# Loads of two heads spread over the projection of v, and sums of x moved past a seam

## The chip, the cores and the metric

The kernel runs on one core of one Trainium2 chip. The metric is the device time of one execution in microseconds (us). The core has five engines that run their own instruction queues and meet by semaphores: TensorE (PE, matmuls into the eight banks of PSUM), VectorE (DVE), ScalarE (ACT), GpSimd (POOL) and SyncE (SP). In this kernel SP computes nothing: its queue issues nearly all transfers between memory and SBUF, one after the other. Sixteen DMA engines carry them out.

## The reference

The input x has 2048 rows and D = 1024 columns. Two attention blocks with 32 heads of 32 columns work on it, and a gate mixes them row by row:

```python
g = _sigmoid((x * gate_w).sum(-1, keepdims=True))
a = _A_ref(x, A_wqkv, A_wo)      # linear attention: pq @ (pk^T v), over pq @ sum(pk)
b = _B_ref(x, B_wqkv, B_wo)      # softmax(q k^T / sqrt(32)) v for each head
return g * a + (1 - g) * b
```

Both blocks first project x by a 1024 x 3072 weight to q, k and v, and finish with a 1024 x 1024 weight. In block A, `phi` makes positive features pq and pk of q and k. All inputs and outputs are float32.

## The kernel before

**Precision.** Every large operand is split into a high and a low part (`split`: a cast on ACT at L293, the rest by a subtraction on DVE at L294), and each product is three matmuls (`three`, L152, L155, L157). A matmul of 128 x 128 by 128 x 512 is the unit of work on TensorE.

**Stage 1, block B's projections.** The rows of x are taken in two halves, J = 0 and J = 1. For each, eight v passes (`v_pass(J, k, ...)`, k = 0 to 7) project 1024 rows to the first 512 columns of v into all eight banks. Eight quads (`quad`) then make q and k, each a 2 x 2 block product by seven products instead of eight, which needs sums and differences of blocks of x (`sides`, four subtractions on DVE at L372 to L375, and `split_sides`, which splits them) and of the weights. The fourth result of `sides`, L375, goes to one of four tiles that also hold results of a quad until `qk<-mid` stores have read them. The results q, k and v go to tensors in memory, `qk` and `v`.

**The seam.** While the last quad of half 0 runs, the generator `change()` (L605) is advanced step by step between its products and prepares half 1: it loads weights of v again, splits the first pieces of x and, in its last step, makes `sides(raw_x1[0], 0)`. The last quad's own last addition on DVE is at L483; it reads the bank of the seventh product, bank 1, which v pass 0 of half 1 fills last. The loop from L628 runs the passes of half 1, and after each pass it issues sums, splits and loads for later passes on DVE, ACT and SP.

**Stage 2, three streams beside each other.** From L921 on, a planner (the loop at the end of the kernel) keeps a modelled clock for each engine and picks the next piece of work from the streams `linear()` (L926), `maxima()` (L1111), `heads_()` and `output()`. All instructions of an engine are queued in the order in which they are picked.

`linear()` goes through units. A unit is one tile of 128 rows (t = 0 to 15) for a chunk of columns: 8 steps k of three matmuls. The first chunk is ("v", 1), the second 512 columns of v of block B, and its 16 units are called unit 0 to 15 here; unit 16 begins block A's k and v. x comes for each unit in two halves of four steps; a half is a pair of transfers (high and low, `big<-xs` or `xh<-xs`, 256 KB each) into one of three places, so half m + 3 is issued when half m has been used (`load_half`). Half m belongs to unit m // 2. At the end of a unit of v, ACT copies its bank (L355) and SP stores it (`v<-mid`).

`maxima()` computes the scores of a head once to find the maximum of each row: one matmul (L1127) and one reduction on DVE (L1132) for each of 64 tiles. Its bulk lies in units 6 to 14, about one matmul to a step. `heads_()` computes the scores again, transposed, with the exponential on ACT (L1301 and L1304); it begins with unit 16.

Head 0 and head 1 need q, k and v in SBUF. `load_q(h, j, j1)` and `load_k(h, j)` issue three transfers each (`big<-qk`, high and low parts of 32 partitions) and, for heads 0 and 1, `memset`s on POOL. `load_head(h)` (L1098) issues all 18 of a head, `load_v(h)` one (`mid<-v`):

```python
            if n == 0:
                load_head(0)
                load_v(0)
            if n == 1:
                load_head(1)
                load_v(1)
```

`gate()` (L487) makes g. Each `next` sums one row tile of x on DVE (L495, a product with `zrep`, which holds the gate's weights) and issues the load of the next row tile (`big<-in_x`, 512 KB). The first `next` loads the weights and row tile 0; the seventeenth sums row tile 15 and goes on to the exponential on ACT (L497) and three small steps on DVE. `linear()` calls it once in each unit of v, at step k = 4, and a second time in unit 15.

In unit 15, as each step of v's weights has been used, the weights of the next chunk are split into their place: a cast on ACT at L728, a subtraction on DVE at L730, from raw tiles loaded by `in_a_wqkv` transfers in pairs.

Of the kernel before, what the change touches and what calls it, by code (L numbers as in the profile page):

```python
# [47 lines left out]
def kernel(  # L48
# [22 lines left out]
    NK = D // P  # L71
    HK = NK // 2
    NT = S // P
    NJ = S // C
# [6 lines left out]
    def f32(ap):  # L81
        return ap.bitcast(F32)
# [37 lines left out]
    def big_tile(i, dtype):  # L120
        return sb.tile([P, S], dtype, name=f"big{i}")
# [39 lines left out]
    def use(eng, cost, *after):  # L161

        T[eng] = max(T[eng], *after, 0.0) + cost
        return T[eng] + LATENCY[eng]

    def dma(to, of):

        T["sp"] = max(T["sp"], T["pe"]) + DMA_ISSUE
        nc.sync.dma_start(to, of)  # L169
# [122 lines left out]
    def split(hi, lo, src, eng):  # L292
        nc.scalar.copy(hi, src)  # L293
        eng.tensor_sub(lo, src, f32(hi))  # L294
# [38 lines left out]
    def xpiece(J, name, p, i):  # L333
        return side_x(J, name, p)[:, i * C:(i + 1) * C]
# [13 lines left out]
    raw_x1 = [raw_a, raw_b, raw_a, raw_b]  # L348
# [20 lines left out]
    def sides(raws, i):  # L369

        r11, r12, r21, r22 = raws
        nc.vector.tensor_sub(r11, r12, r11)  # L372
        nc.vector.tensor_sub(r12, r22, r12)
        nc.vector.tensor_sub(r22, r22, r11)
        nc.vector.tensor_sub(t4_raw[i], r21, r22)  # L375

    def split_sides(raws, J, i):
        r11, r12, _, r22 = raws
        for name, raw in (("T1", r11), ("T2", r22), ("T3", r12)):
            split(xpiece(J, name, 0, i), xpiece(J, name, 1, i), raw, nc.vector)  # L380
# [106 lines left out]
    def gate():  # L487
        xn = halves_of(big_tile(12, F32))
        junk = halves_of(big_tile(13, F32))[0]
        dma(zrep, bass.AP(tensor=gate_w.tensor, offset=gate_w.offset, ap=[[0, P], [1, D]]))  # L490
        for t in range(NT):
            dma(xn[t % 2], x[t * P:(t + 1) * P, :])
            yield
            use("dve", 1.2)
            nc.vector.scalar_tensor_tensor(junk, xn[t % 2], 1.0, zrep, op0=ALU.mult, op1=ALU.mult,  # L495
                                           accum_out=g_sb[:, t:t + 1])
        nc.scalar.activation(g_sb, g_sb, AF.Exp, scale=-1.0)  # L497
        nc.vector.tensor_scalar_add(g_sb, g_sb, 1.0)
        nc.vector.reciprocal(g_sb, g_sb)
        nc.vector.tensor_scalar(omg_sb, g_sb, -1.0, 1.0, op0=ALU.mult, op1=ALU.add)  # L500

    def halves_of(t):
        return [t[:, i * D:(i + 1) * D] for i in range(2)]
# [49 lines left out]
    def load_pair(raws, J, i):  # L553
        for k in (2 * i, 2 * i + 1):
            for jj in range(2):
                load_x(raws, J, jj, k)
# [48 lines left out]
    def change():  # L605

        load_wv_again(range(NK - 1))
        split_x(raw_x1[0], 1, 0, 0)
        yield
        load_wv_again([NK - 1])  # L610
        split_x(raw_x1[0], 1, 1, 0)
        yield
        split_x(raw_x1[0], 1, 0, 1)
        yield
        split_x(raw_x1[0], 1, 1, 1)
        yield
        split_x(raw_x1[1], 1, 0, 2)
        split_x(raw_x1[1], 1, 1, 2)
        yield
        sides(raw_x1[0], 0)  # L620
        split_x(raw_x1[1], 1, 0, 3)
        split_x(raw_x1[1], 1, 1, 3)
        yield
# [4 lines left out]
    for k in range(NK):  # L628
        v_pass(1, k, V_BANKS[1])
        if k == 0:  # L630
            split_sides(raw_x1[0], 1, 0)
            load_pair(raw_x1[2], 1, 2)
            sides(raw_x1[1], 1)
        elif k == 1:
            split_sides(raw_x1[1], 1, 1)
            load_pair(raw_x1[3], 1, 3)
        elif k == 2:
            for kk in (4, 5):
                for jj in range(2):
                    split_x(raw_x1[2], 1, jj, kk)  # L640
            sides(raw_x1[2], 2)
        elif k == 3:
            for kk in (6, 7):
                for jj in range(2):
                    split_x(raw_x1[3], 1, jj, kk)
            sides(raw_x1[3], 3)
            split_sides(raw_x1[2], 1, 2)
            load_quad(raw_a, 0)
            for _ in spill(1, "X12"):
                pass  # L650
        elif k == 4:
            split_sides(raw_x1[3], 1, 3)
            load_quad(raw_b, 1)
        elif k == 5:
            quad_w = quad_weights(raw_a, 1, 0)
            next(quad_w)
            next(quad_w)
        elif k == 6:
            for _ in quad_w:
                pass  # L660
# [265 lines left out]
    def linear():  # L926
        extra = iter(())
        gates = gate()
        for n, (i, t) in enumerate(units):
            kind, c = chunks[i]  # L930
            follow = chunks[i + 1] if i + 1 < len(chunks) else None
# [13 lines left out]
            lin_kind[0] = kind  # L945
            if (kind, c, t) in (("q", 1, 2), ("q", 1, 8), ("o", 0, 2), ("o", 0, 8)):
                load_mix()
            if n == 0:
                load_head(0)
                load_v(0)  # L950
            if n == 1:
                load_head(1)
                load_v(1)
            for k in range(NK):
                yield lambda: ended(w_left[k], w_ready[k], xp_ready.get(2 * n + k // HK, 0.0))
                need(w_left[k])
                stat = [xstat_lin(n, k, p) for p in range(2)]
                for m, _ in enumerate(three(ps, stat, (wpart(k, 0), wpart(k, 1)), k)):
                    lin_pe(1.0)
                    if m < 2:  # L960
                        yield always
                store_mix()
                if kind == "v" and k == NK // 2:
                    next(gates, None)
                    if t == NT - 1:
                        next(gates, None)
                if k % HK == HK - 1:
                    load_half(2 * n + k // HK + 3)
                if k == 0 and n + 7 == len(units) and not o_main[0]:
                    load_o(0)  # L970
                if k == 1 and n + 1 == len(units):
                    assert finished[0] >= H - 2
                    need(pr_left[extra_pr[2]])
                    xo_t[0] = big_tile(PR[extra_pr[2]], F32R)
                    split_o(0, slice(0, NK - 1))
                if k == NK // 2 and n + 1 == len(units) and over["head"]:
                    split_o(1, slice(0, NK - 1))
                if k == NK - 1:
                    yield from extra
                if follow and follow[0] == "o":  # L980
                    if t == NT - 1:
                        w_left[k].clear()
                        yield lambda: 0.0 if mixed.count((k // HK, follow[1])) == 8 * HK else None
                        load_wa(follow[1], k)
                    continue
                if follow and t == NT - 2 and k == 0:
                    yield lambda: None if mix_here or stores else 0.0
                if follow and t == NT - 2 and k < min(LEAD_W, NK):
                    coming_w.append(load_w(*follow, k, LEAD_W + 1))
                if follow and t == NT - 1 and k >= lag:  # L990
                    renew(k - lag)
# [80 lines left out]
    def load_q(h, j, j1=0):  # L1072

        g, r = divmod(h, 4)
        j1 = max(j + 1, j1)
        q, sl = q_cols(h, j, j1), slice(j * C, j1 * C)
        if h < (2 if j else 3):
            nc.gpsimd.memset(f32(q[3 * DH:, :]), 0.0)  # L1078
        else:
            dma(f32(q[3 * DH:3 * DH + 2, :]), f32(q[3 * DH + 2:3 * DH + 4, :]))  # L1080
        for b, p in enumerate((0, 0, 1)):
            dma(f32(q[b * DH:(b + 1) * DH, :]), qk_d[0][p][g][r * DH:(r + 1) * DH, sl])
        for i in range(j, j1):
            q_ready[h][i] = max(T["pe"] + 8.0, T["sp"] + 5.0)

    def load_k(h, j):

        g, r = divmod(h, 4)
        k = k_stack[h % 2]
        if h < 2 and j == 0:  # L1090
            nc.gpsimd.memset(f32(k[3 * DH:, :]), 0.0)
            nc.gpsimd.memset(f32(k[3 * DH:3 * DH + 2, :]), 1.0)
        sl = slice(j * C, (j + 1) * C)
        for b, p in enumerate((0, 1, 0)):
            dma(f32(k[b * DH:(b + 1) * DH, sl]), qk_d[1][p][g][r * DH:(r + 1) * DH, sl])
        k_ready[h][j] = max(T["pe"] + 6.0, T["sp"] + 4.0)

    def load_head(h):  # L1098
        load_q(h, 0)
        load_q(h, 1, NJ)  # L1100
        for j in range(NJ):
            load_k(h, j)

    def v_tile(h):
        return mid[(2, 12)[h % 2]].rearrange("p (t d) -> p t d", d=DH)
# [1 line left out]
    def load_v(h):  # L1107
        c, o = divmod(h * DH, C)
        dma(v_tile(h), v_d[c][:, :, o:o + DH])
# [613 lines left out]
```

## Time and profile before

| what | value |
|---|---|
| median of 3 runs | 2865.99 us (2862.7 to 2868.45) |
| time of the profiled execution | 2866.15 us |
| its span, first to last instruction | 2864.4 us |
| mean granted clock of TensorE | 0.995 |
| TensorE busy | 2825.9 us, 99% of the span |
| DVE, ACT, POOL busy | 2233.2, 1595.8, 1909.2 us |
| mean DMA rate | 150 GB/s |

The profile gives for a group of instructions the line, the engine, the operation and out<-in by tile names; a bracket `[4.32 <-DVE mid L483]` says that the engine stood idle for 4.32 us before this instruction and what released it. A row of the timeline starts with the start and the duration in us; `x18` means that it merges 18 instructions. `SPq` is SP's queue, and the durations there are those of issuing, not of the transfer. A matmul's own duration (0.39 us) is longer than its share of TensorE, since matmuls overlap; the spacing of starts is what counts.

### The profile page before, as it was taken

The numbers are of one execution on the slowest core, as the hardware profiler recorded it, in microseconds if no ns is written. First come the engines' busy times: TensorE is split into PE (matmuls) and PEld (weight loads), VectorE is DVE, ScalarE is ACT, GpSimd is POOL, SyncE is SP. The second block draws the span as 40 slices with busy tenths as digits, with TensorE's granted clock in tenths as the row PEclk, the third lists the DMA queues.
The fourth block names the chain that finished last, engine by engine and source line by source line (L and its number), as shares of the span: only waits on it lengthen the run. The fifth ranks groups of instructions, "written<-read, shape, count | busy, mean of one in ns | idle before, by whom it ended". The sixth has DMA issues, their size and how long they took to land.

```text
span 2864.4 us, 46550 instructions
## 1 busy us (share of the span) xinstructions
PE 2825.9 (99%) x15944; PEld 2058.1 (72%) x15944; DVE 2233.2 (78%) x3659; ACT 1595.8 (56%) x2994; POOL 1909.2 (67%) x894
## 2 busy tenths in 40 slices
PE   9999988899999999999999999999999999999999
PEld 8878877667766776677767777777676766676787
DVE  7767755788888888888888888788888887887522
ACT  5334320366676667666766666566666666666400
POOL 0000010299999999999999999889889888885000
PEclk9999999999999999999999999999999999999999
DMA  8767768533343434333434344455656454634542
GB/s 278 245 214 222 224 202 272 191 87 99 100 133 98 104 100 129 93 96 96 127 107 101 100 122 137 143 173 171 201 174 188 134 163 136 161 108 133 196 151 78
DMA packets 376713, 428.56 MB, mean 150 GB/s; under 512 B 105006, under 2 KB 210734, under 8 KB 376476
## 3 DMA queue, kind: packets, MB, share of 16 engines
q1 hardware_dynamic: 362876, 412.47, 46.9%
q0 software_dynamic: 13600, 13.11, 3.3%
q8 instruction: 127, 2.08, 0.3%
q14 instruction: 110, 0.90, 0.1%
HBM read 298.06 MB, written 112.98 MB: 144 GB/s over the span
## 4 chain that ended last, share of the span: by engine, by line
PE 90%; DMA 2%; SPq 0%; DVE 0%; ACT 0%; issue 0%; ACTq 0%; DVEq 0%
PE bank L1301 17%; PE bank L1127 16%; PE bank L1458 16%; PE bank L152 13%; PE bank L155 13%; PE bank L157 13%; PE bank L1192 1%; PE bank L906 1%; DMA big<-wa 0%; PE bank L795 0%; DMA big<-xs 0%; DMA xh<-xs 0%; SPq L169 0%; DMA big<-qk 0%; PE bank L1184 0%; DMA big<-in_x 0%
## 5 line engine op out<-in xcount | busy, mean ns | idle before, releaser
L1393 POOL TENSOR_TENSOR big<-big,big 128x512 f32<-128x512 f32 (+2 forms) x694 | 1644.2, 2373 | 118.1 <-ACT big L1304 75.5
L1132 DVE TENSOR_REDUCE mx<-bank 128x1 f32<-128x512 f32 x2048 | 1306.8, 683 | 270.6 <-PE bank L1127 266.0
L1304 ACT ACTIVATE big<-bank 128x512 f32<-128x512 f32 x2048 | 1179.2, 601 | 436.3 <-PE bank L1301 367.6
L1301 PE MATMUL bank<-big,big 128*128 128x512 f32 x1888 | 742.5, 395 | 8.3 <-ACT mid L355 7.9
L1127 PE MATMUL bank<-big,big 128*128 128x512 f32 x1888 | 737.9, 392 | 2.8 <-DMA big<-qk 2.8
L152 PE MATMUL bank<-big,big 128*128 128x512 f32 x1600 | 627.4, 392 | 9.6 <-DMA big<-xs 5.2
L155 PE MATMUL bank<-big,big 128*128 128x512 f32 x1600 | 625.4, 391 | 0.0
L157 PE MATMUL bank<-big,big 128*128 128x512 f32 x1596 | 624.0, 391 | 0.3 <-DMA big<-xs 0.3
L1458 PE MATMUL bank<-big,mid 128*32 128x512 f32 x4096 | 454.1, 593 | 0.0
L1301 PEld LDWEIGHTS bank<-big,big 128*128 128x128 f32 x1888 | 354.0, 188 | 134.9 <-issue 47.8
L1127 PEld LDWEIGHTS bank<-big,big 128*128 128x128 f32 x1888 | 354.2, 188 | 77.9 <-issue 3.2
L152 PEld LDWEIGHTS bank<-big,big 128*128 128x128 f32 x1600 | 301.6, 189 | 77.1 <-DMA big<-xs 6.4
L157 PEld LDWEIGHTS bank<-big,big 128*128 128x128 f32 x1596 | 300.7, 188 | 64.9 <-DMA big<-xs 2.4
L155 PEld LDWEIGHTS bank<-big,big 128*128 128x128 f32 x1600 | 301.9, 189 | 63.0 <-DVE big L294 0.2
L1458 PEld LDWEIGHTS bank<-big,mid 128*32 128x32 f32 x4096 | 142.6, 110 | 265.2 <-issue 265.2
L1078 POOL MEMSET big<- 32x512 f32 (+1 forms) x4 | 3.7, 950 | 394.0 <-PE bank L157 394.0
L1409 DVE TENSOR_TENSOR bank<-bank,big 128x512 f32<-128x512 f32 x364 | 251.6, 691 | 5.7 <-ACT big L1304 3.7
L152 PE MATMUL bank<-big,xh 128*128 128x512 f32 x384 | 152.2, 396 | 11.4 <-DMA xh<-xs 10.5
L155 PE MATMUL bank<-big,xh 128*128 128x512 f32 x384 | 151.6, 395 | 0.6 <-DMA big<-wa 0.6
L157 PE MATMUL bank<-big,xh 128*128 128x512 f32 x384 | 151.4, 394 | 0.0
L1389 POOL TENSOR_TENSOR big<-big,big 128x1536 f32<-128x1536 f32 (+1 forms) x31 | 122.4, 3950 | 40.0 <-ACT big L1304 32.9
L293 ACT CAST mid<-mid 128x512 fp32r<-128x512 f32 x64 | 39.7, 621 | 172.6 <-DVE mid L475 74.3
(125 smaller groups left out, 1959.7 us busy)
## 6 DMA issues: line engine op xcount, KB each, us to landing
big<-xs SPq DMA_DIRECT2D x300, 256.0 KB
big<-qk SPq DMA_DIRECT2D x720, 64.0 KB
xh<-xs SPq DMA_DIRECT2D x148, 256.0 KB
qk<-mid SPq DMA_DIRECT2D x128, 256.0 KB
big<-oA SPq DMA_DIRECT2D x84, 256.0 KB
xs<-big SPq DMA_DIRECT2D x64, 256.0 KB
oA<-mid SPq DMA_DIRECT2D x64, 256.0 KB
big<-big POOLq DMA_DIRECT2D x50, 256.0 KB, 5.7
```

Of the source, the lines that this page charges most:

```text
L152: yield nc.tensor.matmul(ps, sh, mh_, start=(kt == 0), stop=False)
L155: yield nc.tensor.matmul(ps, sh, ml_, start=False, stop=(late and last))
L157: yield nc.tensor.matmul(ps, sl, mh_, start=False, stop=last)
L293: nc.scalar.copy(hi, src)
L1127: nc.tensor.matmul(bank[b], q[:, t % TPC * P:(t % TPC + 1) * P], k[:, j * C:(j + 1) * C], start=True, stop=True)
L1132: nc.vector.tensor_reduce(m[:, t, j:j + 1], bank[b], AX.X, ALU.max)
L1301: nc.tensor.matmul(bank[b], k[:, t * P:(t + 1) * P], q_cols(h, j), start=True, stop=True)
L1304: nc.scalar.activation(pr_t[i][:, j * C:(j + 1) * C], bank[b], AF.Exp, scale=SCALE)
L1389: nc.gpsimd.tensor_add(lacc[:, :qp], pr(0)[:, :qp], pr(1)[:, :qp])
L1393: nc.gpsimd.tensor_add(lacc[:, sl], lacc[:, sl], pr(t)[:, sl])
L1409: nc.vector.tensor_add(lacc[:, qp:] if t == NT - 1 else l_b[:, :n], l_b[:, :n], src)
L1458: nc.tensor.matmul(av_b[j * DH:(j + 1) * DH, :], v[:, t, :], pr(t)[:, j * C:(j + 1) * C], start=(t == 0), stop=(t == NT - 1))
```

## The change

In half 1's seam, `sides(raw_x1[0], 0)` leaves the last step of `change()` and is issued after v pass 0, ahead of its `split_sides`. `sides(raw_x1[1], 1)` moves from after v pass 0 to after v pass 1. In the linear stream, `load_head` is dissolved: a queue `first` holds the calls of `load_q`, `load_k` and `load_v` of heads 0 and 1, seven for each head, and one of them is made at every odd step k of the units of v, so the queue is empty after step 3 of unit 3. `gate()` is advanced from unit 2 on, at step 2 of each unit and also at step 6 of odd units.

```diff
@@ change()
         split_x(raw_x1[1], 1, 1, 2)
         yield
-        sides(raw_x1[0], 0)
         split_x(raw_x1[1], 1, 0, 3)
@@ v passes of half 1
         v_pass(1, k, V_BANKS[1])
         if k == 0:
+            sides(raw_x1[0], 0)
             split_sides(raw_x1[0], 1, 0)
             load_pair(raw_x1[2], 1, 2)
+        elif k == 1:
             sides(raw_x1[1], 1)
-        elif k == 1:
             split_sides(raw_x1[1], 1, 1)
@@ linear()
         gates = gate()
+        first = deque()
+        for h in range(2):
+            first.append(lambda h=h: load_q(h, 0))
+            first.append(lambda h=h: load_k(h, 0))
+            first.append(lambda h=h: load_q(h, 1, NJ))
+            first.extend(lambda h=h, j=j: load_k(h, j) for j in range(1, NJ))
+            first.append(lambda h=h: load_v(h))
...
-            if n == 0:
-                load_head(0)
-                load_v(0)
-            if n == 1:
-                load_head(1)
-                load_v(1)
...
-                if kind == "v" and k == NK // 2:
-                    next(gates, None)
-                    if t == NT - 1:
+                if kind == "v":
+                    if k % 2 and first:
+                        first.popleft()()
+                    if t >= 2 and (k == 2 or k == 6 and t % 2):
                         next(gates, None)
```

`load_head` itself is removed.

More of the change, by code (lines that the diff above doesn't have):

```diff
@@ L1096, in load_k @@
         k_ready[h][j] = max(T["pe"] + 6.0, T["sp"] + 4.0)
[L1098 to L1102, printed above, removed]
     def v_tile(h):
```

## The prediction

> **What bounds the kernel now.** I read the page first, for the share of TensorE, then the list of what TensorE waited for, then the busy time in stretches around those waits.
>
> ```profile
> span 2864.4 us, 46550 instructions
> PE 2825.9 (99%) x15944; PEld 2058.1 (72%) x15944; DVE 2233.2 (78%) x3659; ACT 1595.8 (56%) x2994; POOL 1909.2 (67%) x894
> ```
>
> TensorE is busy for 2825.9 of 2864.4 us, so nothing but its gaps can be won here, 38.5 us and whatever a lowered clock adds to them. The list of waits (line, what released it, total us, times, longest) says whose they are:
>
> ```profile
> PE bank L152 <- DMA xh<-xs: 10.5, 2, 9.5
> PE bank L1301 <- ACT mid L355: 7.9, 1, 7.9
> PE bank L152 <- DMA big<-xs: 5.2, 2, 4.5
> PE bank L152 <- DVE mid L483: 4.3, 1, 4.3
> PE bank L1127 <- DMA big<-qk: 2.8, 1, 2.8
> ```
>
> These five sum to 30.7 us. The stretches (start:end, length, then busy us and instructions of each engine, granted clock, DMA share, GB/s) show where they lie and what each place costs with its slow clock:
>
> ```profile
> 200.00:300.00 100.00, 95.68 (x415) 78.73 (x414) 71.65 (x114) 42.34 (x75) 0.00 (x0) 0.98 0.76 236
> 300.00:400.00 100.00, 100.00 (x443) 82.79 (x442) 71.22 (x112) 34.76 (x62) 4.57 (x4) 1.00 0.62 204
> 400.00:450.00 50.00, 32.87 (x122) 25.26 (x121) 13.76 (x23) 4.66 (x8) 6.25 (x5) 0.83 0.78 232
> 450.00:500.00 50.00, 50.00 (x220) 40.66 (x219) 33.63 (x53) 4.70 (x8) 0.00 (x0) 1.00 0.85 287
> 500.00:550.00 50.00, 40.35 (x165) 31.80 (x164) 34.23 (x59) 9.13 (x18) 0.52 (x1) 0.90 0.70 234
> ```
>
> The undisturbed stretch 300 to 400 runs 443 matmuls in 100 us, 0.2257 us each. At that price 415 matmuls are 93.7 us, so the seam loses 6.3 us; 122 are 27.5, so the start of the linear stream loses 22.5 us; 165 are 37.2, so the end of the v chunk loses 12.8 us. That is 41.6 us together, more than the waits because the granted clock falls to 0.83 and 0.90. All three places are touched by the change, and no further group of that list comes to more than 1.1 us. 41.6 us is therefore the most that can be won.
>
> **Part 1: the seam.** On DVE, `sides(raw_x1[0], 0)` (four subtractions, L372 to L375) leaves the last quad and comes after its last addition, L483. `sides(raw_x1[1], 1)` moves from v pass 0 to v pass 1, behind the same neighbours. Nothing is added.
>
> ```profile
> 203.12 9.59 SPq L169 DMA_DIRECT2D qk<-mid  x6
> 203.23 0.68 DVE L372 TENSOR_TENSOR mid<-extra,mid 128x512 f32<-128x512 f32 x1
> 208.45 0.69 DVE L375 TENSOR_TENSOR mid<-xh 128x512 f32<-128x512 f32 x1 [3.08 <-DMA qk<-mid]
> 210.26 0.68 DVE L483 TENSOR_TENSOR mid<-bank,mid 128x512 f32<-128x512 f32 x1
> 211.00 0.50 PE L152 MATMUL bank<-big,big 128*128 128x512 f32 x1 [4.32 <-DVE mid L483]
> 219.90 1.33 DVE L294 TENSOR_TENSOR big<-xh,big 128x512 fp32r<-128x512 f32 x2
> ```
>
> L375 overwrites a tile that a store of the quad is still reading, so DVE stands for 3.08 us; L483 stands behind it, and the v pass waits for the bank that L483 reads. Without the four sums, DVE at 203.23 does two splits (1.3 us) and then L483, which ends near 205.2. TensorE asks for the bank at 206.68 (211.00 less 4.32). The cover is 1.5 us, and if it fails the price is what it fails by. L375 still waits for its store until 208.45, but what stands behind it then is only the splits of the sums, which the quads use some 40 us later, and the next loads of x. Those give the pieces of v pass 4, split at 219.90 now; TensorE comes to pass 4 at 211.0 + 0.9 + 3 x 5.42 + 2 (slow clock) = 230, and 6.3 us sooner after the change, 224. Their order on DVE does not get later, so some 3 us of cover stay. Gain 6.3 us; bounds 0 (L483 still late) and 6.3.
>
> **Part 2: the first transfers of the v chunk.** Before, unit 0 issues 18 loads of q and k and one of v for head 0 in one go on SP's queue, unit 1 the same for head 1, and the halves of x that TensorE needs next stand behind them. After, the same 38 transfers come in 14 portions of one or three, at odd steps k of units 0 to 3; the gate's weights and rows start in unit 2 instead of 0. Nothing is added or removed.
>
> ```profile
> 407.85 8.43 SPq L169 DMA_DIRECT2D big<-qk  x18
> 417.01 1.73 SPq L169 DMA_DIRECT2D big<-xs  x2
> 421.35 0.80 PE L152 MATMUL bank<-big,big 128*128 128x512 f32 x1 [4.53 <-DMA big<-xs]
> 421.75 11.99 SPq L169 DMA_DIRECT2D big<-qk  x18
> 434.46 1.72 SPq L169 DMA_DIRECT2D xh<-xs  x2
> 439.60 0.80 PE L152 MATMUL bank<-big,xh 128*128 128x512 f32 x1 [9.49 <-DMA xh<-xs]
> 439.64 0.57 SPq L169 DMA_DIRECT2D big<-in_x  x1
> 461.43 0.59 ACT L355 COPY mid<-bank 128x512 f32<-128x512 f32 x1 [4.85 <-DMA big<-xs]
> 404.50 1.81 POOL L1092 MEMSET big<- 2x2048 f32 x1
> ```
>
> TensorE waits for half 3, issued at 417.01 behind the first batch, and for half 5, issued at 434.46 behind the second, which lands 5.1 us after its issue. The waits would vanish if issuing were free, but it isn't: from 407.85 to the end of the row at 439.64 SP issues 54 transfers (36 of q and k, 2 of v, 10 of x, the gate's weights, 3 rows, 2 stores of v) in 32.4 us, 0.60 us each. In the changed order 65 transfers stand from the first load of q to the second of half 11, the last that unit 5 needs (36, 2, 18, the gate's weights, 4 rows, 4 stores). At 0.60 us they end at 446.8; half 11 is issued 1.2 us sooner, lands 5.1 us later, at 450.7, and 12 matmuls of 0.2257 us end unit 5 at 453.4. Before, the copy at 461.43 marks the same end. Gain 8.0 us. The upper bound takes the pace of the first batch, 8.43 / 18 = 0.468 us (pair of half 11 at 437.4, end of the unit at 445.1, gain 16); the lower one that of the second, 11.99 / 18 = 0.666 us (449.8, 457.7, gain 4). I take 8, since the 0.60 is the mean over the same mixture. So the two long waits become several of 1 to 3 us, for halves 3, 7, 8 and 9, and the first maxima run after unit 1, when their loads have landed.
>
> The eight memsets on POOL keep their total and have POOL to themselves; the last ends at 406.3 ahead of the first load, and the splitting only reorders them: nothing.
>
> On bytes instead of transfers, the Trainium skill ("DMA: Bandwidth & Descriptors", section "Where 436 GB/s comes from") gives some 358 GB/s as the limit of one core's memory side; the 65 transfers hold 12.1 MB, so by it they would be done in 34 us, unit 5 would end near 444, and the sum of all parts would be about 2834, an estimate from that page. No stretch quoted here comes near that rate; the highest is 287 GB/s, from 450 to 500.
>
> **Part 3: the gate's rows.** After unit 2 every unit issues one row at step 2 and odd units another at step 6, so the last row is summed in unit 13 and no row lies in units 14 to 16. A row's transfer and its L495 keep their price; there are 16 as before.
>
> ```profile
> 459.32 0.38 SPq L169 DMA_DIRECT2D big<-in_x  x1
> 465.67 1.23 DVE L495 SCALAR_TENSOR_TENSOR big<-big,zrep 128x1024 f32<-128x1024 f32 x1 [5.18 <-DMA big<-in_x]
> 530.87 0.97 SPq L169 DMA_DIRECT2D mid<-in_a_wqkv  x2
> 534.54 0.33 SPq L169 DMA_DIRECT2D big<-in_x  x1
> 535.28 1.08 SPq L169 DMA_DIRECT2D extra<-in_a_wqkv  x2
> 540.38 1.23 DVE L495 SCALAR_TENSOR_TENSOR big<-big,zrep 128x1024 f32<-128x1024 f32 x1 [6.57 <-DMA big<-in_x]
> 541.64 0.22 ACT L497 ACTIVATE g_sb<-g_sb 128x16 f32<-128x16 f32 x1 [13.37 <-DVE big L495]
> 543.83 0.57 ACT L355 COPY mid<-bank 128x512 f32<-128x512 f32 x1
> 544.46 0.79 PE L1301 MATMUL bank<-big,big 128*128 128x512 f32 x1 [7.91 <-ACT mid L355]
> ```
>
> The chain reads upward from the last line: TensorE waits for the copy of unit 15's bank, which stands on ACT behind the gate's exponential, which waits for the last L495, which waits for a row issued at 534.54. After the change the copy stands only behind the six first splits of the next weights. The sixth's raw tile is issued at 530.87; at 4.3 us (417.01 to 421.35) to 5.1 us it lands at 535.2 to 536.0, and a split of 0.6 and the copy of 0.57 free the bank near 537. TensorE asks at 536.55, and some 1.7 us sooner without two small waits for x just before: a wait of 2 us stays. Behind it the eighth raw tile, issued at 535.28, lands near 540; the first exponentials of head 0 stand behind its split on ACT, and TensorE, with six steps of unit 16 to do meanwhile, waits another 1.5 to 2 us. Of 12.8 us lost some 3.8 stay: gain 9.0. Bounds: 12.8 (the splits hidden), and 4 if the weights land 5 us later.
>
> Where the rows go: in units 7, 9 and 11 two rows lie 4 steps apart, with a maxima matmul in each step 16 x 0.2257 = 3.6 us, while a row took 6.35 us from issue (459.32) to L495 (465.67). DVE then stands up to 2.7 us, and reductions of maxima behind it hold banks. At 465.67 DVE had stood for 5.18 us and no wait of TensorE followed, so I take 0; the bound is 3 x 2.7 = 8 us. The gate's exponential, now in unit 13, has its row a whole unit old: nothing.
>
> **Sum.** 6.3 + 8.0 + 9.0 = 23.3 us. The profiled execution took 2866.15 us, 1.75 over its span and 0.16 over the median of the runs, so the forecast is 2842.8, say 2843. With the bounds of the terms alone (0 / 4 / 4 less 8, and 41.6) it could be anything from 2825 to 2866; the rivals sort these.
>
> **Rivals.** (a) All three places close wholly: 2866.15 - 41.6 = 2824.6. For it: the first batch's pace of 0.468 us. Against: even at that pace part 2 gives 16 of its 22.5 us, and part 3 keeps two splits in the way.
>
> (b) The burst only moves. Halves, rows, q, k and v are the same transfers on one queue, and unit 5 ends where it did: part 2 gives 0, and the time is 2866.15 - 15.3 = 2850.9. For it: the second batch went at 0.666 us with hardly anything between. Against: from 430.1 to 439.6 TensorE stood while only q, k and v were issued, and in the new order halves come between them. The Trainium skill speaks for (b): by "DMA: Bandwidth & Descriptors", section "Issuing engines are not separate DMA queues", all transfers share 16 engines and interleave wherever they are issued. The trace agrees in part: the share of the engines was 0.78 over 400 to 450, so there is room, but not much.
>
> (c) The tail's wait is taken over by the weights (bound 4 of part 3): 2866.15 - 18.3 = 2847.9. For it: six splits stand ahead of the copy in either order. Against: a megabyte of rows less on the way just there.
>
> (d) Slower: rows starve the halves in units 6 to 12.
>
> ```profile
> big<-in_x SPq DMA_DIRECT2D x10, 512.0 KB
> big<-xs SPq DMA_DIRECT2D x26, 256.0 KB
> v<-mid SPq DMA_DIRECT2D x10, 256.0 KB
> ```
>
> A unit there moves four pieces of x, a store and 1.5 rows, 2.1 MB in 32 x 0.2257 = 7.2 us, or 291 GB/s, against one row and 255 GB/s before. To end 5.7 us over the old time the seven units must give back 23.3 + 5.7 = 29 us, 4.1 each: the engines would have to bring only 2.1 MB in 11.3 us, 186 GB/s. From 450 to 500 they brought 287 at a share of 0.85. At such a point the time would be 2872.
>
> (e) The seam stays open because L483 is late all the same: 2849.
>
> **How the numbers follow.** Forecast 0.50, (a) 0.12, (b) 0.18, (c) 0.12, (d) 0.05, (e) 0.03. The forecast's own range is 2836 to 2848: part 2 between 4 and 14. From 2829 to 2854 the range takes in (b), (c) and (e) with 3 us for the spread of the runs and leaves (a) and (d) out, 0.17. A measurement can tell 0.2% from no change, 5.7 us; slower is (d), 0.05; within 0.2% I put 0.04, the part of (b) where two rows in odd units cost the bound of 8 us too; the rest, 0.91, is faster.
>
> **What would show it.** Seam: L483 ends before L372 starts, and the list of waits has no L152 <- DVE L483. Part 2: no batch of 18 on SP, halves issued between portions of 3, waits for x of 1 to 3 us instead of 4.5 and 9.5, and the copy of unit 5 some 14 us earlier (8 and the seam's 6). Part 3: L497 in unit 13, L355 of unit 15 directly behind splits, a wait under 3 us where 7.9 stood. I am wrong if unit 5's copy comes less than 10 us sooner, if TensorE waits for DVE in units 7, 9 or 11, or if a new wait of over 5 us stands at the first exponentials.

## The result and the profile after

The changed kernel takes 2852.77 us (median of 5 runs, 2852.39 to 2854.43) against 2865.99 us before (5 runs, 2862.7 to 2868.45): a ratio of 0.9956, 95% interval 0.9941 to 0.9971. It is faster by 13.2 us. That lies in the wide range of 2829 to 2854, which takes in rivals, but 4.8 us above the forecast's own range of 2836 to 2848. The forecast was a gain of 23 us; where the other 10 went is the question of this part.

The page and the list of TensorE's waits of the changed kernel:

```profile
span 2852.0 us, 46554 instructions
PE 2823.2 (99%) x15944; PEld 2055.9 (72%) x15944; DVE 2232.2 (78%) x3659; ACT 1597.9 (56%) x2994; POOL 1910.0 (67%) x894
...
PE bank L152 <- DMA big<-xs: 18.2, 5, 8.9
PE bank L1123 <- ACT big L1300: 2.4, 2, 1.5
...
PE bank L1297 <- ACT mid L355: 0.5, 1, 0.5
```

The wait on DVE at the seam is gone, and the 7.9 us behind the gate have become 0.5. But TensorE still waits 18.2 us for halves of x, one of them for 8.9 us; before, it was 10.5 + 5.2. The stretches say the same:

```profile
200.00:300.00 100.00, 100.00 (x443) 82.84 (x442) 75.16 (x119) 43.54 (x76) 0.00 (x0) 1.00 0.80 248
400.00:450.00 50.00, 32.61 (x112) 23.58 (x111) 8.73 (x14) 2.35 (x4) 0.00 (x0) 0.81 0.90 238
450.00:500.00 50.00, 50.00 (x218) 41.27 (x217) 39.56 (x64) 4.25 (x8) 0.00 (x0) 0.98 0.89 307
500.00:550.00 50.00, 45.75 (x198) 36.09 (x197) 38.37 (x67) 20.05 (x39) 8.75 (x5) 1.00 0.64 210
```

The seam now runs its full 443 matmuls in 100 us, and 500 to 550 has 198 instead of 165. From 400 to 450 there are 112 where there were 122, with the DMA engines busy for 0.90 of the time instead of 0.78.

ACT's copy at L355 marks the end of each unit of v. In the changed kernel those of units 0, 5, 14 and 15 are

```profile
402.72 0.59 ACT L355 COPY mid<-bank 128x512 f32<-128x512 f32 x1 [2.78 <-PE bank L157]
...
457.25 0.59 ACT L355 COPY mid<-bank 128x512 f32<-128x512 f32 x1 [5.06 <-PE bank L157]
...
522.63 0.59 ACT L355 COPY mid<-bank 128x512 f32<-128x512 f32 x1 [6.67 <-PE bank L157]
...
532.50 0.58 ACT L355 COPY mid<-bank 128x512 f32<-128x512 f32 x1
```

and before they were

```profile
409.47 0.59 ACT L355 COPY mid<-bank 128x512 f32<-128x512 f32 x1 [2.79 <-PE bank L157]
...
526.33 0.59 ACT L355 COPY mid<-bank 128x512 f32<-128x512 f32 x1 [6.67 <-PE bank L157]
```

(461.43 and 543.83 for units 5 and 15 stand in the prediction). The lead is 6.8 us at unit 0, 4.2 at unit 5, 3.7 at unit 14 and 11.3 at unit 15. So the seam gave its part, units 0 to 5 gave 2.6 us back instead of winning 8, and the end of the chunk gave 7.6. Behind unit 15 another 1 to 2 us follow (the two spans differ by 12.4 us, the medians by 13.2); there the granted clock from 540 to 550 was 0.52 before and is 1.00 now.

What SP's queue did in units 0 to 4 of the changed kernel, with the wait of 8.9 us on TensorE behind it:

```profile
401.10 2.73 SPq L169 DMA_DIRECT2D big<-qk  x6
...
413.75 0.59 SPq L169 DMA_DIRECT2D mid<-v  x1
414.40 3.67 SPq L169 DMA_DIRECT2D big<-qk  x3
...
421.26 0.46 SPq L169 DMA_DIRECT2D zrep<-in_gate_w  x1
421.77 0.42 SPq L169 DMA_DIRECT2D big<-in_x  x1
...
424.70 0.96 SPq L169 DMA_DIRECT2D big<-xs  x2
425.71 8.40 SPq L169 DMA_DIRECT2D big<-qk  x6
434.51 1.10 SPq L169 DMA_DIRECT2D xh<-xs  x2
...
438.07 0.57 SPq L169 DMA_DIRECT2D mid<-v  x1
438.74 4.05 SPq L169 DMA_DIRECT2D big<-xs  x2
...
434.49 0.80 PE L152 MATMUL bank<-big,big 128*128 128x512 f32 x1 [8.86 <-DMA big<-xs]
```

The first six loads are issued in 2.73 us, 0.46 each. Later it is three in 3.67 us, six in 8.40, two in 4.05: SP itself stands. What SP's queue waited for between 425 and 435 us:

```profile
SPq L169 <- DMA big<-in_x: 2.3, 1, 2.3
SPq L169 <- DMA zrep<-in_gate_w: 2.0, 1, 2.0
SPq L169 <- DMA big<-qk: 1.9, 3, 0.8
```

In the program each transfer waits for the semaphore that the transfer eight places earlier signals, so a transfer that lands slowly holds the queue. From the first load of q at 401.10 to the last piece of half 11 at 446.74 the 65 transfers took 0.70 us each, not the 0.60 of the prediction. The half that TensorE waits 8.9 us for, half 7, was issued at 424.70, behind the gate's weights and a row, and was there at 434.49, some 9.8 us later.

Two theories could explain this. Theory S says that it is a matter of order: halves of x stand behind loads on one queue. Theory E says that it is the engines: they are full in units 0 to 5 with whatever is given to them there.

### The profile page after: what moved, and what is told of

It is laid out like the page before. It is cut to its first block, busy times and chain, and to the rows that moved or that the text cites. A ratio compares the mean times of both kernels' runs of the same rounds, so it can differ in the third digit from the quotient of the medians.

```text
span 2852.0 us, 46554 instructions
## 1 busy us (share of the span) xinstructions
PE 2823.2 (99%) x15944; PEld 2055.9 (72%) x15944; DVE 2232.2 (78%) x3659; ACT 1597.9 (56%) x2994; POOL 1910.0 (67%) x894
## 4 chain that ended last, share of the span: by engine, by line
PE 96%; DMA 2%; SPq 0%; issue 0%; ACT 0%; DVE 0%; POOL 0%; ACTq 0%
PE bank L1297 17%; PE bank L1123 16%; PE bank L152 15%; PE bank L1454 15%; PE bank L155 15%; PE bank L157 15%; DMA big<-xs 1%; PE bank L1188 1%; PE bank L906 1%; PE bank L795 0%; DMA v<-mid 0%; SPq L169 0%; DMA big<-qk 0%; PE bank L1180 0%; DMA big<-wa 0%
## 5 line engine op out<-in xcount | busy, mean ns | idle before, releaser
L152 PE MATMUL bank<-big,big 128*128 128x512 f32 x1600 | 627.5, 392 | 18.3 <-DMA big<-xs 18.2
L1463 ACT COPY mid<-bank 128x512 f32<-128x512 f32 x32 | 18.8, 588 | 207.5 <-PE bank L1454 207.5
```

The costliest lines, as they stand in the source:

```text
L152: yield nc.tensor.matmul(ps, sh, mh_, start=(kt == 0), stop=False)
```

## The experiments

Each line gives the median, and from the profile the time from unit 0's copy to unit 5's. The kernel before was run again beside the experiments, with medians of 2866.25 to 2866.91 us, and the ratios below are against these. Only one execution of each kernel was profiled; it stands up to 2.4 us off the median, and in one pair below a unit that the edit does not touch differs by 1.5 us. The kernel with ACT's queue and the three wide ones run seven maxima, 1.6 us, in unit 6 that the others run in units 0 to 5.

| kernel | median us | unit 0 to 5, us |
|---|---|---|
| before | 2866.0 | 52.0 |
| the change | 2852.8 | 54.5 |
| seam alone | 2860.3 | 50.6 |
| seam and spread loads | 2861.7 | 54.2 |
| seam and gate rows | 2848.1 | 50.2 |
| change, q and k on ACT's queue | 2853.3 | 45.8 |
| change, v late | 2847.5 | 46.0 |
| seam, gate rows, bursts, v late | 2848.2 | 48.0 |
| change, rows from unit 5 | 2848.5 | 44.1 |
| change, v late, other 256 KB in v's place | 2848.6 | 48.3 |
| wide placement | 2840.7 | 35.5 |
| wide, v in units 16 and 18 | 2840.4 | 36.4 |
| wide, v in units 1 and 3 | 2843.9 | 43.7 |

**The parts one by one.** First the seam's edit alone, which is the first two hunks of the diff.

> The kernel before with the seam's edit alone (sums of x moved). If the seam's gain is kept to the end: TensorE's wait on DVE's L483 is gone, unit 0's copy comes 6 to 7 us sooner, and the time is near 2860. Rival: the burst of unit 0 waits for something that did not move, and gives the gain back by unit 5: 2865 to 2866.

Measured: 2860.27 us, ratio 0.9976 (0.9967 to 0.9985). The gain of 6.0 us is kept, as the first theory said.

Then the spread loads without the new places of the gate:

```diff
-                if kind == "v":
-                    if k % 2 and first:
-                        first.popleft()()
-                    if t >= 2 and (k == 2 or k == 6 and t % 2):
+                if kind == "v" and k % 2 and first:
+                    first.popleft()()
+                if kind == "v" and k == NK // 2:
+                    next(gates, None)
+                    if t == NT - 1:
                         next(gates, None)
```

> The seam's edit and the spread loads, with the gate's rows as before (step 4 of each unit, two in unit 15). Theory E, the DMA engines bound units 0 to 5 in any order: spreading alone gives nothing, the wait of 7.9 us behind the gate stays, time 2859 to 2862. Theory S, order on SP's queue bounds them and only the rows of units 3 and 5 spoilt it: unit 5's copy near 449, time near 2852.

Measured: 2861.73 us, 0.9982 (0.9973 to 0.9991), 1.5 us behind the seam alone, where the intervals overlap. Spreading gained nothing, without the second rows too. That is theory E's case. Up to 450 us the waits for halves fell from 11.7 us to 10.1 against the seam alone, but the first maxima's wait for q and k rose from 3.0 to 5.8.

And the gate's rows without the spread loads (`load_head` and `load_v` in units 0 and 1 as before, the seam's edit and the new `next(gates)`):

> The seam's edit and the new places of the gate's rows, with the loads of heads 0 and 1 in two bursts as before. If the tail carries the gain that the changed kernel shows: the wait at the end of the v chunk falls from 7.9 to under 3 us, time 2850 to 2853, as the changed kernel or better. Theory S expects the two long waits for x to stay and the time above the changed kernel's, 2856 or more, since the spread loads would be worth something.

Measured: 2848.06 us, 0.994 (0.9926 to 0.9953): 12.2 us better than the seam alone and 4.7 better than the whole change. So the spread loads are the part of the change that costs time. The two long waits for x stayed, as theory S expected, at 5.9 and 4.7 us, but its time of 2856 or more did not come. The list of waits of this kernel between 515 and 560 us:

```profile
PE bank L152 <- DMA big<-xs: 1.9, 1, 1.9
PE bank L1126 <- ACT big L1303: 0.3, 1, 0.3
```

The 7.9 us for the copy behind the gate are gone (7.5 with the seam alone). The 1.9 for a half is not new: the kernel before has 1.0 and 0.7 there.

**Order or engines.** The changed kernel with the 36 loads of q and k on another queue:

```diff
+    def dma_act(to, of):
+        nc.scalar.dma_start(to, of)
...
-            dma(f32(q[b * DH:(b + 1) * DH, :]), ...)
+            (dma_act if h < 2 else dma)(f32(q[b * DH:(b + 1) * DH, :]), ...)
```

(and the same in `load_k`).

> The changed kernel with the 36 loads of q and k for heads 0 and 1 issued on ScalarE's queue instead of SP's, in the same places. Theory S (halves of x stand on SP's queue behind loads that wait for earlier transfers to land): waits of TensorE for x in units 1 to 4 fall from 15 us to under 6, time near 2843. Theory E (the engines are full): waits stay at 12 us or more, time 2850 to 2855.

Measured: 2853.31 us, 0.9955 (0.9942 to 0.9967): the same as the change. Waits for x up to 450 us:

```profile
PE bank L152 <- DMA big<-xs: 12.3, 3, 7.5
PE bank L152 <- DMA xh<-xs: 2.2, 1, 2.2
PE bank L157 <- DMA big<-xs: 1.8, 3, 0.8
PE bank L157 <- DMA xh<-xs: 1.3, 1, 1.3
```

They come to 17.6 us, against 17.3 in the change. With q and k out of their way on SP, TensorE waited as long for the halves. ACT was held up in its turn:

```profile
399.71 10.42 ACTq L1075 DMA_DIRECT2D big<-qk  x12
410.17 0.59 ACT L355 COPY mid<-bank 128x512 f32<-128x512 f32 x1 [9.92 <-DMA big<-qk]
```

(Unit 0's copy stands on ACT behind these loads and came 7 us later for that, so the 45.8 us in the table do not mean a gain; unit 5's copy stands at 455.95, against 457.25.) Theory S falls as far as q and k are the loads that the halves stand behind. The Trainium skill's rule ("DMA: Bandwidth & Descriptors", section "Issuing engines are not separate DMA queues") is that the transfers share the same engines, whoever issues them. It held here: 2853.3 us against 2852.8.

**The dear loads: v.** A load of v for a head takes 32 columns out of 512, 256 KB in pieces of 128 bytes.

```diff
-            first.append(lambda h=h: load_v(h))
...
+                    if k == 1 and t in (13, 14):
+                        load_v(t - 13)
```

> The changed kernel with the two loads of v of heads 0 and 1 (256 KB each, in pieces of 128 bytes) moved from units 1 and 3 to units 13 and 14. If the small pieces are what fills the engines in units 1 to 4: the waits for x there fall from 17 us to under 10 and the time is near 2846. If the q and k loads fill them: waits of 14 us or more, 2850 to 2853. A wait of over 3 us in units 13 to 15 would say that their price only moved.

Measured: 2847.48 us, 0.9932 (0.992 to 0.9945), 5.3 us better than the change. Units 0 to 5 took 46.0 instead of 54.5 us. The part that was feared came too, a wait of 3.6 us for x in unit 15 where the change has 1.8.

To tell pieces from bytes, the same kernel with a transfer of 256 KB in pieces of 2 KB in v's old places (its contents are overwritten by the later load of v):

```diff
+                    if (t, k) in ((1, 5), (3, 3)):
+                        dma(v_tile(t // 2).rearrange("p t d -> p (t d)"), v_d[0][:, t, :])
```

> The changed kernel with the two loads of v in units 13 and 14, and in their old places in units 1 and 3 transfers of the same 256 KB into the same tiles in pieces of 2 KB, whose contents are overwritten later and used for nothing. If the small pieces are dear and not the bytes: within 2 us of the kernel with v late (2847.5). If it is bytes, or one more transfer in the row: back at 2851 to 2853.

Measured: 2848.57 us, 0.9936 (0.9923 to 0.9948), 1.1 us behind the kernel with v late. Units 0 to 5 took 48.3 us, 2.3 more than with nothing there and 6.2 less than with v. So it is mainly the small pieces. What they do can be read while the first of the two is on its way, from its issue for some 5 us (it has landed at 418.70) in the change, and for some 4 us in the kernel with pieces of 2 KB (the tail of each line is clock, DMA share, GB/s):

```profile
413.75:418.75 5.00, 4.39 (x18) 3.02 (x17) 2.77 (x5) 0.00 (x0) 0.00 (x0) 1.00 0.93 193
```

```profile
416.25:420.25 4.00, 2.97 (x12) 1.84 (x11) 1.89 (x3) 0.00 (x0) 0.00 (x0) 1.00 0.86 266
```

With v the engines bring 193 GB/s at a share of 0.93, with the larger pieces 266 at 0.86. The Trainium skill says of this ("DMA: Bandwidth & Descriptors", section "Specifications") that pieces of at least 512 bytes are needed for the full rate. The runs agree in direction; they did not test a piece of 512.

The small pieces also hold SP's queue. The transfer issued right behind the load, in the change and in the kernel with pieces of 2 KB:

```profile
413.75 0.59 SPq L169 DMA_DIRECT2D mid<-v  x1
414.40 2.74 SPq L169 DMA_DIRECT2D big<-qk  x1
```

```profile
416.26 0.42 SPq L169 DMA_DIRECT2D mid<-v  x1
416.73 0.43 SPq L169 DMA_DIRECT2D big<-qk  x1
```

Behind the second load it is 3.48 us (the first half of the row at 438.74 above) against 0.45. The profile puts most of that 3.48 down to TensorE, but the place that this transfer fills had been used by 425.6. So the loads of v hold up what stands behind them on the queue as well as filling the engines. Which of the two the stage pays for is not shown: v on another queue was not tried, and that form of theory S stays open.

With the loads of q and k in bursts, v late gives much less:

> Seam, the gate's rows in their new places, the loads of q and k in two bursts as before, and the two loads of v in units 13 and 14. If small pieces of v are the dear part, this gains on the bursts with v (2848.1) what the spread kernel gains by the same edit, some 6 us: near 2842. If they are cheap: 2847 to 2849.

Measured: 2848.22 us, 0.9933 (0.9921 to 0.9946), as the bursts with v in place (2848.1). Units 0 to 5 fell by 2.2 us, from 50.2 to 48.0, and unit 15 took that back: unit 14's copy to unit 15's is 11.9 us (516.75 to 528.67) instead of 10.3 (518.93 to 529.19). The edit that is worth 8.5 us to units 0 to 5 in the spread order is worth 2.2 in the bursts. Without v in the stage the two orders come out alike, 2847.5 us spread and 2848.2 in bursts; with v they are 2852.8 and 2848.1. So what the spread order lost is what the loads of v cost more in it, and spreading q and k by itself neither gained nor lost. Why v costs less behind a burst was not settled. The issue behind it is shorter there (1.33 and 1.55 us in the kernel with the seam and the gate rows), and TensorE stands there anyway for the halves behind it; both would fit, and no run separates them.

**The rows.** The changed kernel with the gate's rows, and with them its weights, from unit 5 on:

```diff
-                    if t >= 2 and (k == 2 or k == 6 and t % 2):
+                    if t >= 5 and (k == 2 or k == 6 and t > 5):
```

> The changed kernel with the gate's rows starting in unit 5 and two in every unit from 6 on, so that only q, k, v and x are on the way in units 2 to 4. If the rows of units 2 to 5 are what made the spread loads worse than the bursts: unit 5's copy comes 6 us sooner than in the changed kernel and the time is near 2847. If not: 2851 to 2855.

Measured: 2848.49 us, 0.9933 (0.9921 to 0.9946), 4.3 us better. Unit 5's copy came at 446.81, 10.4 us sooner, more than expected; units 5 to 15 then took 81.6 us (446.81 to 528.45) against 75.3 in the change, since they carry the rows. So v is not the only load that matters: what is taken out of units 1 to 4, rows and gate weights or small pieces, shortens them, and what is put into later units costs less there, but not nothing.

**A version that beats both.** The wide placement takes as much as possible out of units 0 to 5:

```diff
-            first.append(lambda h=h: load_v(h))
+        slots = [(t, k) for t in range(3) for k in (3, 7)] + [(11, 5), (12, 3), (12, 5), (12, 7), (13, 1), (13, 3)]
...
-                    if k % 2 and first:
+                    if (t, k) in slots:
                         first.popleft()()
-                    if t >= 2 and (k == 2 or k == 6 and t % 2):
+                    if 3 <= t <= 13 and (k == 2 or k == 6 and 6 <= t <= 11):
                         next(gates, None)
+                    if t == 14 and k == 1:
+                        load_v(0)
```

(v of head 1 follows in unit 17.)

> The changed kernel with less in units 0 to 5: head 0's q and k in six portions at steps 3 and 7 of units 0 to 2, head 1's in units 11 to 13, v of head 0 in unit 14 and of head 1 in unit 17; one row in units 3 to 5, 12 and 13, two in units 6 to 11. Theory E (the engines bound units 0 to 5 by what they carry there): about half of the q, k and v load and some rows leave the stage, waits for x in units 1 to 5 fall under 6 us and the time to 2835 to 2842. Theory S, order alone: no more than 2 us under the changed kernel. Against both: two rows in units 6 to 11 could make TensorE wait for DVE or x there, which this run would show.

Measured: 2840.73 us, 0.9909 (0.9894 to 0.9924), 12.0 us under the change and 26 under the kernel before. Its waits up to 450 us:

```profile
PE bank L152 <- DMA big<-xs: 1.9, 2, 1.0
PE bank L152 <- DMA xh<-xs: 1.2, 1, 1.2
PE bank L157 <- DMA xh<-xs: 0.7, 1, 0.7
PE bank L157 <- DMA big<-xs: 0.6, 2, 0.4
```

4.4 us in place of 17.3. Of the 19 us by which units 0 to 5 became shorter, 1.6 are seven maxima that moved to unit 6, and some came back later: from unit 14's copy to unit 15's it is 14.3 us (507.47 to 521.81).

That last wait was put down to v in unit 14, and v moved again:

```diff
-                    if t == 14 and k == 1:
-                        load_v(0)
-                if (kind, c, t, k) == ("kv", 0, 1, 1):
-                    load_v(1)
+                if (kind, c, k) == ("kv", 0, 2) and t in (0, 2):
+                    load_v(t // 2)
```

> The wide placement with both loads of v after the v chunk, in units 16 and 18, where the transfers of the stage have room. If the load of v in unit 14 holds the halves of unit 15: the wait of 3.9 us for x there goes and the time falls by 4 us, near 2837. If the next chunk's weights hold them: no change from 2840.7.

Measured: 2840.39 us, 0.9906 (0.9892 to 0.9919): no change, as the second expectation has it. In the profile unit 15 is shorter by 2.8 us (508.73 to 520.27), but unit 14 longer by 0.6 and unit 4, which the edit does not touch, by 1.5, so a small gain may hide in the spread of the executions. The wait for x in unit 15 went from 3.9 us to 1.9. The next chunk's weights are the likely rest of unit 15's length, which is argued and not shown: ACT's split of the sixth waits for its raw tile, and the copy follows directly.

```profile
519.75 0.62 ACT L728 CAST big<-mid 128x512 fp32r<-128x512 f32 x1 [2.16 <-DMA mid<-in_a_wqkv]
520.27 0.58 ACT L355 COPY mid<-bank 128x512 f32<-128x512 f32 x1
```

Last, v back in units 1 and 3 of the wide kernel (`if (t, k) in ((1, 5), (3, 3)): load_v(t // 2)`):

> The wide placement with the two loads of v back in units 1 and 3, as in the changed kernel. If a load of v costs 4 us wherever the stage is tight, because of its pieces of 128 bytes: unit 5's copy comes 6 to 9 us later than in the wide kernel, time 2843 to 2847 (with the unit 15's wait saved). If it only hurt together with the q, k and rows beside it: at most 2 us later, time 2837 to 2840.

Measured: 2843.87 us, 0.992 (0.9907 to 0.9934), 3.5 us more. Units 0 to 5 took 7.4 us longer than with v in 16 and 18 (43.7 against 36.4). So the small pieces cost the stage 7 to 8 us even where rows, q and k are thinned out. Of that 3.5 us are left in the whole time.

## Why the prediction was right and where it was wrong

**Part 1, the seam: right.** 6.3 us forecast, 6.0 measured by itself. L483 runs before the sums, as said:

```profile
203.91 0.68 DVE L483 TENSOR_TENSOR mid<-bank,mid 128x512 f32<-128x512 f32 x1
205.33 0.69 DVE L294 TENSOR_TENSOR mid<-mid,mid 128x512 fp32r<-128x512 f32 x1 [0.73 <-ACT mid L293]
205.94 0.68 DVE L372 TENSOR_TENSOR mid<-extra,mid 128x512 f32<-128x512 f32 x1
...
208.11 0.69 DVE L375 TENSOR_TENSOR mid<-xh 128x512 f32<-128x512 f32 x1
```

L375 did not even have to wait for its store any more.

**Part 2, the spread loads: wrong.** Forecast a gain of 8.0 us with bounds of 4 and 16; measured a loss, 1.5 us with the old gate and 4.7 with the new. By the prediction's own sign, unit 5's copy less than 10 us sooner, its mechanism failed: the copy came 4.2 us sooner. The step that failed is "0.60 us each" as the price of issuing. An issue that waited for nothing took some 0.46 us (six in 2.73); most of the rest of the 0.60, and of the 0.70 that came, was waiting, and this order did not remove it. From 401 to 447 SP waited 8.9 us for transfers to land, and 2.3 us more went into the issue behind the first load of v. The second batch's 0.666 us, which I took for the lower bound, was no bound either.

Two further terms of that step failed with it. A half was to land 5.1 us after its issue; half 7 took some 9.8. And half 11 was to set the end of unit 5; TensorE did not wait for it at all, and what made unit 5 late were the 8.9 us for half 7 and 3.4 for half 9. That the 65th transfer ended at 446.74, as the sum's 446.8, is chance: the sum left out the seam's lead of 6.8 us, with which it should have ended near 440.

Rival (b), that the burst only moves, named the mechanism and gave it 0.18; its evidence, an engine share of 0.78 over 400 to 450, I read as room. The other point against it was misread: from 430.1 to 439.6 not only q, k and v were issued, but from 434.46 on halves of x and a row as well. In the change the share was near 1 for much of units 1 to 4, and it brought few bytes:

```profile
427.50:430.00 2.50, 0.00 (x0) 0.00 (x0) 0.00 (x0) 0.00 (x0) 0.00 (x0) 0.57 1.03 192
```

against 388 GB/s at 1.05 in the kernel before:

```profile
425.00:427.50 2.50, 2.50 (x8) 1.77 (x7) 1.24 (x2) 0.24 (x1) 0.00 (x0) 0.65 1.05 388
```

No load of v was on its way in that stretch of the change. The gate's weights, a row, half 7 and loads of q were, and the rows from unit 5 on, which take the weights and rows out, made unit 3 5.0 us shorter (14.1 against 19.1). Why these bytes came so slowly was not taken apart. The estimate from the Trainium skill's 358 GB/s ("DMA: Bandwidth & Descriptors", section "Where 436 GB/s comes from") went wrong the same way: the changed kernel brought 238 GB/s at a share of 0.90 from 400 to 450, so that limit was far off, and the engines were full all the same. Nor was it a limit here, with 388 GB/s over 2.5 us in the kernel before. The prediction knew of the two loads of v and counted each as one transfer in 65; the runs price them at 7 to 8.5 us of the stage together in the spread order.

**Part 3, the gate: right.** Forecast 9.0 with a bound of 12.8. The new places gave 9.0 us on top of the spread loads (2861.73 to 2852.77) and 12.2 on top of the bursts. The medians' intervals are some 2.6 us wide to either side for the seam alone and 3.7 for the kernel with the gate rows, so the two do not differ clearly. The profiles of the latter pair give about 10, 8.0 between the copies of units 14 and 15 (18.3 to 10.3) and 2.1 behind them, where the granted clock from 540 to 550 was 0.87 and became 1.00. Of the two waits that were to stay, 2 us for the copy and 1.5 to 2 for the exponentials, the change shows 0.5 and 1.5, and the one for a half just before, 1.8, which I had thought gone. That two rows in odd units would cost nothing held: TensorE waited for no L495 in units 7, 9 or 11, and units 6 to 14 took 65.4 us (457.25 to 522.63) against 64.9 before (461.43 to 526.33).

**Rivals.** (a) would have needed the spread to work. (c) did not come. (d) did not come: from 450 to 500 the engines brought 307 GB/s and TensorE ran without a wait. (e) did not come.

Put one on top of the other, the parts are 6.0 + 12.2 - 4.7 = 13.5 us, and the change gave 13.2 in its own comparison; this is a sum of steps between the same medians and no test of them. The forecast was 23.3 because its middle term was +8.0 and not -4.7.

That the time stayed in the range of 2829 to 2854 was luck as far as part 2 goes. The range had been drawn wide enough for rivals (b), (c) and (e), and a loss was in none of part 2's bounds.

## What to carry to other kernels

When the gaps between issues on a DMA queue are long, ask first how much of them is waiting for earlier transfers to land. Here much of it was, and spreading transfers over the same stretch won nothing, while moving them out of it did. Price a transfer by its pieces too, and not only by its bytes or by its count: a strided load of 128-byte pieces was among the dearest things in a stage full of 256 KB blocks. And a stage that waits should be relieved of what is not due there: the loads of head 1, of v and most of the rows were due tens of microseconds later.

## What the runs showed of the hardware that was not expected

- Two loads of 256 KB in pieces of 128 bytes cost a tight stage 7.4 and 8.5 us where the loads were spread and 2.2 where they came in bursts; two of the same size in pieces of 2 KB cost 2.3 us.
- The transfer issued right behind such a load took 1.25 us or more to issue, 2.74 and 3.48 in the change; behind pieces of 2 KB it took 0.43 and 0.45.
- The busy share of the DMA engines says little on bytes: shares just over 1 stood beside 192 and 388 GB/s, and 0.90 and 0.89 beside 238 and 307.
- Issuing 36 of the loads on another engine's queue changed the time by 0.5 us, within the noise.
